# The opening loads of an attention-plus-SwiGLU kernel over two queues, batch 1's v on the GpSimd queue, and the shared tail tile moved in block 1

## The chip, the cores and the metric

The kernel runs on one core of one Trainium2 chip. The metric is device time in microseconds (us), the median of several executions. One more execution was recorded by the hardware profiler, and all views of the profile come from that one.

A core has five instruction streams: TensorE (PE, with its weight loads as PEld), VectorE (DVE), ScalarE (ACT), GpSimd (POOL) and SyncE (SP). Each stream runs in order and waits on semaphores. A DMA is issued by one of these streams and then moves its data by itself; the stream goes on.

## The reference

Linear attention with cosine weights, then an RMS norm and a SwiGLU feed-forward, in float32:

```python
# q, k, v: (8 batches, 8 heads, 576 rows, 64)
r = np.maximum(x, 0.0); phi(x) = np.concatenate([r * cos_w, r * sin_w], -1)   # 128 features
kv  = np.einsum('bhsf,bhsd->bhfd', k_p, v);  z = np.sum(k_p, axis=2)
num = np.einsum('bhsf,bhfd->bhsd', q_p, kv)
den = np.einsum('bhsf,bhf->bhs', q_p, z)[..., None] + 1e-06
x   = (num / den).transpose(0, 2, 1, 3).reshape(4608, 512)
xn  = x / sqrt(mean(x * x) + 1e-6) * rms_g
out = (silu(xn @ w_gate) * (xn @ w_val)) @ w_out      # 512 -> 1536 -> 512
```

## The kernel before

**Tiling.** Each batch has 576 rows: 512 main rows, held as four tiles of 128 rows (c or j = 0 to 3), and a tail of 64 rows. The tails of two neighbouring batches share one 128-row tile (c or j = 4). The feed-forward works in blocks: block b holds the 512 main rows of batch b, and block 8 holds all tails. A block has 12 steps n (`gval_step`, lines 663 to 670: eight 512-column matmuls for gate and value, the Silu `sg` on ACT, the product `hT` on DVE), and then 4 output steps, numbered 12 to 15 (`out_step`, lines 672 to 680: 12 matmuls with `wo`, a copy to `osb` on ACT, a store by SP). Gate and value use PSUM banks n % 2, so step n needs what ACT and DVE read in step n - 2.

**Attention of batch nb**, spread over the steps of earlier blocks: `k_phi` and `q_phi` (lines 218 to 242) scale and clip k and q, cosine half on DVE, sine half on ACT; `v_cast` (275) converts v to bf16, heads 0 to 3 (LOW) and 4 to 7 (HIGH); `kvz_pe` (293) makes kv and z, 40 matmuls in head order into PSUM tile `psA`; `kvz_evac` copies them to `kvzs`; `nd_pe` (308) makes numerator and denominator of one row tile from the transposed q (`qpT`, for the tail `qtT`); `nd_post` (331) divides, on DVE; `x_sq` squares and sums on ACT and takes the power -1/2 on POOL; `x_norm` (362) makes the bf16 `xn` on DVE; a transpose then makes `xnT`, the moving operand of the feed-forward. Transposes go through PE in the opening and for batch 1, and through DMAs issued by SP (`q_tr_dma`, 253; `x_tr_dma`, 382) from batch 2 on.

**What sets the order.** The schedule is written by hand. `at(blk, n, where, f, ...)` (line 583) hangs a piece of work on step n of block blk: "pe" ahead of that step's matmuls, "pre" after them, "post" after ACT's and DVE's part. Each engine's stream follows this order. The scheduling framework adds the semaphore waits.

**The opening** (lines 117 to 133 and 446 to 569). SP issues all loads of batch 0, in the order k LOW, k HIGH, k tail, q (row pairs 0 and 1 of 4), v LOW, v tail, v heads 4 and 5, v heads 6 and 7, q (pairs 2 and 3), `rms_g`. PE runs filler matmuls until data is there. POOL issues six weight loads (`gval_slice`, 457; they read float32 and write bf16), the first of which waits for v's tail (line 462). `kvz` of batch 0 goes to `psA`, and its first half is copied out by ACT while PE waits to go on with the second half in the same tile.

**Batch 1** (`first_loads_of_1`, 592). SP issues k, gated on the fifth weight load (594), then q, then v in two halves and its tail. POOL issues four loads of `wo`, the first gated on q (line 607). Block 0's output matmuls (717) need `wo` and are mixed with batch 1's attention.

**Batch 2** is the "late" one (lines 623 to 654): its attention runs inside block 1, the block just before it is needed. Before the change `v_cast` is at steps 3 and 4, `q_phi` with `q_tr_dma` at steps 5 to 7, `kvz` at step 7, `nd` of the four row tiles at steps 8, 10, 12 and 13, each tile's `x_norm` and transpose one step later. The shared tail of batches 0 and 1 is at step 6 (lines 734 to 743): `q_phi` of the two tails at steps 2 and 3, `nd_pe(1, 4)` at step 6. Later batches have a fixed pattern that the change leaves alone.

Of the kernel before, what the change touches and what calls it, by code (L numbers as in the profile page):

```python
# [22 lines left out]
def kernel(  # L23
# [11 lines left out]
    nc = tc.nc  # L35
# [3 lines left out]
    P = 128  # L39
# [20 lines left out]
    )  # L60
    psO = ps_open.tile([P, 2, 512], FP32, name="psO")

    nc.scalar.preload_act_table(AF.Silu)

    V, A, G = nc.vector, nc.scalar, nc.gpsimd
    LOW, HIGH = (0, 4), (4, 8)
# [1 line left out]

    raw = {}

    def load_main(which, src, b, heads=(0, 8), bufs=one):
        key = (which, b)
        if key not in raw:
            raw[key] = bufs.tile([P, H, 4 * D], FP32, name=f"r{which}", tag=f"r{which}")
        h0, h1 = heads
        return nc.sync.dma_start(  # L76
            out=raw[key][:, h0:h1, :],
            in_=src[b, h0:h1, 0:512, :].rearrange("h (p j) d -> p h (j d)", j=4),
        )

    def load_tail(which, src, b):
        t = two.tile([P, 4, D], FP32, name=f"r{which}t", tag=f"r{which}t")
        raw[(which + "t", b)] = t
        for g in range(2):
            d = nc.sync.dma_start(  # L85
                out=t[64 * g : 64 * g + 64, :, :],
                in_=src[b, 4 * g : 4 * g + 4, 512:576, :].rearrange("h s d -> s h d"),
            )
        return d
# [16 lines left out]
    def load_pair(which, b, jj):  # L106
# [5 lines left out]
        return nc.sync.dma_start(  # L112
            out=raw[key][:, :, jj * 2 * D : (jj + 1) * 2 * D],
            in_=view[:, :, 2 * jj : 2 * jj + 2, :].rearrange("p h j d -> p h (j d)"),
        )

    first = {}
    load_main("k", k, 0, LOW, two)
    load_main("k", k, 0, HIGH, two)
    load_tail("k", k, 0)  # L120
    load_pair("q", 0, 0)
    load_main("v", v, 0, LOW)
    first["v"] = load_tail("v", v, 0)
    load_main("v", v, 0, (4, 6))
    load_main("v", v, 0, (6, 8))
    load_pair("q", 0, 1)

    gb = one.tile([P, DM], FP32, name="gb")
    with nc.allow_non_contiguous_dma(reason="rms_g to all partitions"):
# [113 lines left out]

    def q_dst(b, c):
        if (b, c // 4) not in qpT:
            qpT[(b, c // 4)] = two.tile(
                [P, H, 512] if c < 4 else [P, 4, P], BF16,
                name="qpT" if c < 4 else "qtT", tag="qpT" if c < 4 else "qtT",
            )
        t = qpT[(b, c // 4)]  # L250
        return t[:, :, c * P : (c + 1) * P] if c < 4 else t[:, :, :]
# [17 lines left out]
    def copy(eng, o, i):  # L269
        if eng is nc.scalar:  # L270
            nc.scalar.copy(out=o, in_=i)  # L271
        else:
            eng.tensor_copy(out=o, in_=i)
# [19 lines left out]
    def kvz_pe(b, pst, heads=range(8)):  # L293
        o = headview(pst)
        for h in heads:
            for c in range(5):
                lhsT = kp_main[b][:, c, h, :] if c < 4 else kpt[b % 2][:, h % 4, :]
                rhs = vvm[b % 2][:, c, h, :] if c < 4 else vvt[b % 2][:, h, :]
                nc.tensor.matmul(  # L299
                    o[:, h // 4, h % 4, :], lhsT=lhsT, rhs=rhs, start=(c == 0), stop=(c == 4)  # L300
                )

    def kvz_evac(eng, b, pst, bank):
        if b not in kvzs:
            kvzs[b] = two.tile([P, 2, 4 * E], BF16, name="kvzs", tag="kvzs")
        copy(eng, kvzs[b][:, bank, :], pst[:, bank, 0 : 4 * E])

    def nd_pe(b, j, pst):

        o = headview(pst)  # L310
        for h in range(H):
            g, i = h // 4, h % 4
            if j < 4:
                nc.tensor.matmul(  # L314
                    o[:, g, i, :], lhsT=qpT[(b, 0)][:, h, j * P : (j + 1) * P],
                    rhs=kvzs[b][:, g, i * E : (i + 1) * E], start=True, stop=True,
                )
            else:
                for bb in (b - 1, b):
                    lo = 64 * (bb % 2)  # L320
                    nc.tensor.matmul(
                        o[lo : lo + 64, g, i, :],
                        lhsT=qpT[(bb, 1)][:, i, 64 * g : 64 * g + 64],
                        rhs=kvzs[bb][:, g, i * E : (i + 1) * E], start=True, stop=True,
                    )

    x_of = {}
# [129 lines left out]
    def gval_slice(c0, c1):  # L457
# [2 lines left out]

    gval_slice(0, 256)
    tc.add_manual_dep(
        weight_dmas[0].ins, first["v"].ins.name, SYNC_DEP, reason="weights after v"
    )
    gval_slice(256, 768)
    gval_slice(768, 1536)
# [8 lines left out]
    v_cast(A, 0, LOW)  # L475
    v_cast_tail(A, 0)
    filler(2, idle)
    kvz_pe(0, psA, range(0, 4))
    filler(1, idle)
    v_cast(V, 0, (4, 6))  # L480
    v_cast(V, 0, (6, 7))
    v_cast(A, 0, (7, 8))
    kvz_evac(A, 0, psA, 0)
    kvz_pe(0, psA, range(4, 6))
    filler(1, idle)
    kvz_pe(0, psA, range(6, 8))
    filler(2, idle)
    kvz_evac(V, 0, psA, 1)
    for c in (2, 3):
        q_phi(A, 0, c, 1)  # L490
    nd_pe(0, 0, psA)
# [42 lines left out]
    x_tr_pe(0, 0, psG[1][:, :])  # L534
    x_tr_evac(V, 0, 0, psG[1][:, :])
    x_norm(0, 1)
    filler(1, idle)
    open_ffn(0, (0, 1), 0, 128)
    x_tr_pe(0, 1, psG[1][:, :])
# [43 lines left out]
    def at(blk, n, where, f, *args):  # L583
        slots.setdefault((blk, n), none())[where].append((f, args))
# [7 lines left out]
    def first_loads_of_1():  # L592
        d = load_main("k", k, 1, bufs=two)
        tc.add_manual_dep(d.ins, weight_dmas[4].ins.name, SYNC_DEP, reason="after the weights")
        load_tail("k", k, 1)
        gate = load_main("q", q, 1)
        load_main("v", v, 1, LOW)
        load_main("v", v, 1, HIGH)
        load_tail("v", v, 1)
        for i in range(4):  # L600
            d = nc.gpsimd.dma_start(
                out=wo[:, 3 * i : 3 * i + 3, :],
                in_=moe_w_out[3 * i * P : 3 * (i + 1) * P, :].rearrange("(t p) m -> p t m", p=P),
            )
# [18 lines left out]
    for nb in range(2, B):  # L623
        b = nb - 1
        late = nb == 2
        for c in range(5):
            kb, kn = (b, (c + 1) // 2) if late else (b - 1, 12 + (c * 3) // 5)
            at(kb, kn, "post", k_phi, V, nb, c, 0)
            at(kb, kn, "post", k_phi, A, nb, c, 1)
            qn = 5 + (c * 3) // 5 if late else c  # L630
            at(b, qn, "post", q_phi, V, nb, c, 0)
            at(b, qn, "post", q_phi, A, nb, c, 1)
            at(b, qn, "post", q_tr_dma, nb, c)
        vb, vn = (b, 3) if late else (b - 1, 14)
# [145 lines left out]
```

## Time and profile before

| | |
|---|---|
| median of 6 runs | 339.29 us (337.63 to 340.56) |
| the profiled execution | 342.04 us, of which the recorded span is 340.3 us |
| PE busy | 323.4 us, 95% of the span |
| DVE, ACT, POOL busy | 181.3, 169.4, 37.9 us |
| mean granted TensorE clock | 0.985 of full speed |
| DMA | 54.14 MB, mean 159 GB/s |

How to read it: the 1.74 us between the profiled execution's time and its span lie outside the recorded instructions. PE's busy share counts pipelined matmuls, and a matmul at half clock is as busy as one at full clock, so 95% hides both kinds of loss; the waits of PE and the granted clock by stretch show them. Times inside the trace are counted from the start of the span. A DMA's "landing" is the time from its issue to its completion semaphore.

### The profile page before, as it was taken

Reading aid. Unit: us, or ns where it says so; the run is one execution under the profiler, and the core shown is the slowest. Engines: PE = TensorE matmul, PEld = TensorE weight load, DVE = VectorE, ACT = ScalarE, POOL = GpSimd, SP = SyncE. Lnnn points to the kernel's source line nnn. Section 1 sums busy time; section 2 is a strip of 40 time slices with the busy share of each in tenths; the row PEclk is TensorE's granted clock in tenths of the full one; section 3 lists DMA queues with packets and bytes.
Section 4 is the critical chain, followed back from the end, with each engine's and each line's share of the span. In section 5 each row is a group of like instructions: output and inputs, shape, how many; then the busy total and the mean of one; then the engine's idle time right before and its main releaser. Section 6 shows DMA issues by size and latency. Waiting matters only on the chain.

```text
span 340.3 us, 5906 instructions
## 1 busy us (share of the span) xinstructions
PE 323.4 (95%) x2157; PEld 164.4 (48%) x2193; DVE 181.3 (53%) x372; ACT 169.4 (50%) x327; POOL 37.9 (11%) x83
## 2 busy tenths in 40 slices
PE   8989999879969999999999999999999999999994
PEld 3578455535423544454445444544454444444441
DVE  4675747575842576558635765575368323304410
ACT  5655844746443645654565465546554333223321
POOL 3520302101110011101100120011001100000000
PEclk9999999989996999999999999999999999999999
DMA  8999999949693966897759776977551320020014
GB/s 232 270 206 272 266 174 280 329 116 165 164 249 79 212 163 160 209 208 193 201 153 234 175 199 152 227 180 206 151 86 35 90 77 1 2 96 27 2 31 93
DMA packets 94957, 54.14 MB, mean 159 GB/s; under 512 B 59984, under 2 KB 90192, under 8 KB 94928
## 3 DMA queue, kind: packets, MB, share of 16 engines
q1 hardware_dynamic: 90160, 49.04, 58.3%
q0 software_dynamic: 4768, 4.72, 8.4%
q8 instruction: 17, 0.28, 0.4%
q14 instruction: 12, 0.10, 0.1%
HBM read 38.01 MB, written 9.44 MB: 139 GB/s over the span
## 4 chain that ended last, share of the span: by engine, by line
PE 82%; DMA 8%; issue 2%; DVE 2%; ACT 2%; SPq 2%; POOL 0%; ACTq 0%; DVEq 0%; POOLq 0%
PE psG L403 25%; PE psV L403 25%; PE psC L423 23%; PE psA L299 3%; DMA rq<-in_q_dram 3%; PE psA L314 2%; DMA wo<-in_moe_w_out_dram 2%; DMA rv<-in_v_dram 2%; DMA xnT<-xn 1%; PE psG L423 1%; SPq L85 1%; DMA qtT<-qp 1%; SPq L76 1%; ACT scr L352 1%; DVE xt L340 1%
## 5 line engine op out<-in xcount | busy, mean ns | idle before, releaser
L418 DVE TENSOR_TENSOR hT<-psV,sg 128x512 bf16<-128x512 f32 x102 | 70.3, 690 | 107.5 <-PE psV L403 79.0
L403 PE MATMUL psG<-xnT,wg 128*128 128x512 bf16 (+1 forms) x353 | 93.2, 382 | 5.0 <-DMA xnT<-xn 3.1
L412 ACT ACTIVATE sg<-psG 128x512 f32<-128x512 f32 x102 | 60.6, 594 | 74.1 <-PE psG L403 69.0
L403 PE MATMUL psV<-xnT,wv 128*128 128x512 bf16 (+1 forms) x364 | 94.0, 380 | 0.6 <-issue 0.2
L423 PE MATMUL psC<-wo,hT 128*128 128x512 bf16 x394 | 90.8, 379 | 1.0 <-DMA wo<-in_moe_w_out_dram 0.5
L403 PEld LDWEIGHTS <-wv 128*128 128x128 bf16 x416 | 41.3, 99 | 49.3 <-issue 3.2
L423 PEld LDWEIGHTS <-hT 128*128 128x128 bf16 x432 | 41.3, 98 | 48.2 <-DMA wo<-in_moe_w_out_dram 0.6
L403 PEld LDWEIGHTS <-wg 128*128 128x128 bf16 x416 | 39.1, 99 | 46.4 <-issue 3.9
L357 POOL TENSOR_TENSOR rs<-ms,mhalf 128x1 f32<-128x1 f32 x36 | 20.0, 554 | 207.7 <-ACT scr L352 207.7
L271 ACT COPY osb<-psC 128x512 f32<-128x512 f32 x33 | 19.4, 587 | 46.8 <-PE psC L423 46.8
L352 ACT ACTIVATE scr<-xt 128x513 bf16<-128x513 f32 x36 | 22.9, 635 | 25.0 <-DVE xt L340 24.0
L364 DVE SCALAR_TENSOR_TENSOR xn<-xt,rs,gb 128x512 bf16<-128x512 f32 x36 | 27.4, 760 | 14.1 <-POOL rs L357 13.9
L340 DVE TENSOR_TENSOR xt<-psA,rec 128x512 f32<-128x512 f32 x35 | 24.2, 691 | 1.2
L212 ACT ACTIVATE qp<-rq,tab 128x512 bf16<-128x512 f32 x32 | 22.2, 712 | 2.2 <-DMA rq<-in_q_dram 2.2
L212 ACT ACTIVATE kpm<-rk,tab 128x512 bf16<-128x512 f32 (+1 forms) x34 | 21.1, 675 | 2.4 <-DMA rk<-in_k_dram 2.4
L214 DVE TENSOR_SCALAR kpm<-rk,tab 128x512 bf16<-128x512 f32 (+1 forms) x38 | 15.2, 451 | 3.2 <-DMA rk<-in_k_dram 3.2
L314 PEld LDWEIGHTS <-qpT 128*128 128x128 bf16 x256 | 12.3, 98 | 8.0 <-issue 1.4
L214 DVE TENSOR_SCALAR qp<-rq,tab 128x512 bf16<-128x512 f32 x32 | 15.2, 488 | 0.6 <-DMA rq<-in_q_dram 0.6
L443 PE MATMUL psG<-warm 128*128 128x512 bf16 x47 | 13.8, 439 | 1.2 <-DVE fidx L149 1.2
L314 PE MATMUL psA<-kvzs,qpT 128*128 128x65 bf16 x248 | 13.0, 194 | 0.6 <-DVE xt L340 0.3
L403 PE MATMUL psG<-xnt_tail,wg 128*128 128x512 bf16 x48 | 12.3, 379 | 0.1
L403 PE MATMUL psV<-xnt_tail,wv 128*128 128x512 bf16 x47 | 12.1, 379 | 0.0
(82 smaller groups left out, 191.4 us busy)
## 6 DMA issues: line engine op xcount, KB each, us to landing
out_dram<-osb SPq DMA_DIRECT2D x32, 256.0 KB, 2.8
rv<-in_v_dram SPq DMA_DIRECT2D x22, 256.0 KB, 3.5
rk<-in_k_dram SPq DMA_DIRECT2D x20, 256.0 KB, 3.4
rq<-in_q_dram SPq DMA_DIRECT2D x20, 256.0 KB, 3.1
rk<-in_k_dram SPq DMA_DIRECT2D x2, 1024.0 KB, 7.2
rq<-in_q_dram SPq DMA_DIRECT2D x2, 1024.0 KB, 9.2
rv<-in_v_dram SPq DMA_DIRECT2D x3, 512.0 KB, 9.5
wo<-in_moe_w_out_dram POOLq DMA_DIRECT2D x4, 384.0 KB, 7.2
```

Of the source, the lines that this page charges most:

```text
L212: nc.scalar.activation(out=out_ap, in_=in_ap, func=AF.Relu, scale=scale)
L214: eng.tensor_scalar(out=out_ap, in0=in_ap, scalar1=scale, scalar2=0.0, op0=ALU.mult, op1=ALU.max)
L271: nc.scalar.copy(out=o, in_=i)
L314: nc.tensor.matmul(o[:, g, i, :], lhsT=qpT[(b, 0)][:, h, j * P : (j + 1) * P], rhs=kvzs[b][:, g, i * E : (i + 1) * E], start=True, stop=True,)
L340: nc.vector.tensor_tensor(out=xt[:, 0:DM].rearrange("p (b h d) -> p b h d", b=2, d=D), in0=o[:, :, :, 0:D], in1=rec[:, :, :].unsqueeze(3). ...
L352: nc.scalar.activation(out=scr[:, :], in_=xt[:, 0 : DM + 1], func=AF.Square, scale=1.0 / math.sqrt(DM), accum_out=ms[:, :],)
L357: nc.gpsimd.tensor_tensor(out=rs[:, :], in0=ms[:, :], in1=mhalf[:, :], op=ALU.pow)
L364: nc.vector.scalar_tensor_tensor(out=xn[:, :], in0=x_of[(b, j)][:, 0:DM], scalar=rs_of[(b, j)][:, :], in1=gb[:, :], op0=ALU.mult, op1=ALU. ...
L403: nc.tensor.matmul(pst[bank][:, cols[0] : cols[1]], lhsT=w[:, t, n * P : (n + 1) * P], rhs=x[:, t, cols[0] : cols[1]], start=(t == 0), sto ...
L412: nc.scalar.activation(out=sg[:, :], in_=psG[bank][:, :], func=AF.Silu)
L418: nc.vector.tensor_tensor(out=hTs[blk][:, n, :], in0=psV[bank][:, :], in1=sg[:, :], op=ALU.mult)
L423: nc.tensor.matmul(bank, lhsT=hTs[blk][:, n, j * P : (j + 1) * P], rhs=wo[:, n, :], start=(n == 0), stop=(n == NNT - 1),)
```

## The change

Four things change together.

1. The loads of k, q and v of batch 0 are split by heads: LOW halves stay on SP's queue, HIGH halves are issued by ACT on its own queue. The loading of ACT's function table, which stood first on ACT, now follows ACT's three DMA issues. The first weight load waits for ACT's half of q instead of v's tail.
2. `kvz` of batch 0 goes to two separate PSUM banks, and both halves are copied out at the end, one by ACT and one by DVE. `kvzs` becomes two tiles per batch, with three buffers each.
3. v of batch 1 (two halves and its tail) is issued by POOL, between the second and third power instruction of batch 0's norm, instead of by SP after q. `wo` is still gated on q.
4. In block 1 batch 2 moves forward: `v_cast` to steps 2 and 3, `q_phi` with its transposes to steps 3 to 5, `kvz` to step 5, `nd` to steps 6, 8, 10 and 12. The shared tail's `nd` moves from step 6 to output step 14, with its norm and transpose at 15; `qtT` has four buffers instead of two.

The numbers of PE, DVE and ACT compute instructions are the same. In the opening SP issues 9 loads instead of 12 and ACT issues 3; four loads of batch 1 move from SP to POOL.

```diff
-    nc.scalar.preload_act_table(AF.Silu)
...
-    def load_main(which, src, b, heads=(0, 8), bufs=one):
+    def load_main(which, src, b, heads=(0, 8), bufs=one, queue=nc.sync):
...
     load_main("k", k, 0, LOW, two)
-    load_main("k", k, 0, HIGH, two)
+    load_main("k", k, 0, HIGH, two, A)
     load_tail("k", k, 0)
-    load_pair("q", 0, 0)
+    load_pair("q", 0, 0, nc.sync, LOW)
+    first["q"] = load_pair("q", 0, 0, A, HIGH)
     load_main("v", v, 0, LOW)
-    first["v"] = load_tail("v", v, 0)
-    load_main("v", v, 0, (4, 6))
-    load_main("v", v, 0, (6, 8))
+    load_main("v", v, 0, HIGH, queue=A)
+    load_tail("v", v, 0)
     load_pair("q", 0, 1)
+    nc.scalar.preload_act_table(AF.Silu)
...
-            qpT[(b, c // 4)] = two.tile(
+            qpT[(b, c // 4)] = (two if c < 4 else four).tile(
...
     tc.add_manual_dep(
-        weight_dmas[0].ins, first["v"].ins.name, SYNC_DEP, reason="weights after v"
+        weight_dmas[0].ins, first["q"].ins.name, SYNC_DEP, reason="weights after q"
     )
...
-    kvz_pe(0, psA, range(0, 4))
+    kvz_half(0, half_view[0], range(0, 4))
     filler(1, idle)
...
-    kvz_evac(A, 0, psA, 0)
-    kvz_pe(0, psA, range(4, 6))
+    kvz_half(0, half_view[1], range(4, 6))
     filler(1, idle)
-    kvz_pe(0, psA, range(6, 8))
+    kvz_half(0, half_view[1], range(6, 8))
     filler(2, idle)
-    kvz_evac(V, 0, psA, 1)
+    kvz_half_evac(A, 0, half_view[0], 0)
+    kvz_half_evac(V, 0, half_view[1], 1)
...
     x_norm(0, 1)
+    load_main("v", v, 1, LOW, queue=G)
+    load_main("v", v, 1, HIGH, queue=G)
+    load_tail("v", v, 1, G)
...
         gate = load_main("q", q, 1)
-        load_main("v", v, 1, LOW)
-        load_main("v", v, 1, HIGH)
-        load_tail("v", v, 1)
...
-            qn = 5 + (c * 3) // 5 if late else c
+            qn = 3 + c // 2 if late else c
...
-        vb, vn = (b, 3) if late else (b - 1, 14)
+        vb, vn = (b, 2) if late else (b - 1, 14)
...
-        kz, nds = (7, (8, 10, 12, 13)) if late else (4, (5, 7, 9, 11))
+        kz, nds = (5, (6, 8, 10, 12)) if late else (4, (5, 7, 9, 11))
...
-    at(1, 6, "pe", nd_pe, 1, 4, psA)
-    at(1, 6, "pre", nd_post, 1, 4, psA)
-    at(1, 6, "post", x_sq, 1, 4)
-    at(1, 7, "post", x_norm, 1, 4)
-    at(1, 7, "post", x_tr_dma, 1, 4)
+    at(1, 14, "pe", nd_pe, 1, 4, psA)
+    at(1, 14, "pre", nd_post, 1, 4, psA)
+    at(1, 14, "post", x_sq, 1, 4)
+    at(1, 15, "post", x_norm, 1, 4)
+    at(1, 15, "post", x_tr_dma, 1, 4)
```

`kvz_half` is `kvz_pe` with one bank's four heads (h % 4) in a view of `psG[1]` (LOW) or `psV[1]` (HIGH).

More of the change, by code (lines that the diff above doesn't have):

```diff
@@ L75, in load_main @@
         h0, h1 = heads
-        return nc.sync.dma_start(
+        return queue.dma_start(
             out=raw[key][:, h0:h1, :],
@@ L79, in load_main, with load_tail @@
         )
-    def load_tail(which, src, b):
+    def load_tail(which, src, b, queue=nc.sync):
         t = two.tile([P, 4, D], FP32, name=f"r{which}t", tag=f"r{which}t")
@@ L84, in load_tail @@
         for g in range(2):
-            d = nc.sync.dma_start(
+            d = queue.dma_start(
                 out=t[64 * g : 64 * g + 64, :, :],
@@ L104, in load, with load_pair @@
         last_load[(which, b)] = load_tail(which, src_of[which], b)
-    def load_pair(which, b, jj):
+    def load_pair(which, b, jj, queue=nc.sync, heads=(0, 8)):
         key = (which, b)
@@ L111, in load_pair @@
         view = src_of[which][b, :, 0:512, :].rearrange("h (p j) d -> p h j d", j=4)
-        return nc.sync.dma_start(
-            out=raw[key][:, :, jj * 2 * D : (jj + 1) * 2 * D],
-            in_=view[:, :, 2 * jj : 2 * jj + 2, :].rearrange("p h j d -> p h (j d)"),
+        return queue.dma_start(
+            out=raw[key][:, heads[0] : heads[1], jj * 2 * D : (jj + 1) * 2 * D],
+            in_=view[:, heads[0] : heads[1], 2 * jj : 2 * jj + 2, :].rearrange(
+                "p h j d -> p h (j d)"
+            ),
         )
@@ L303, in kvz_evac, with kvz_half, kvz_half_evac @@
     def kvz_evac(eng, b, pst, bank):
-        if b not in kvzs:
-            kvzs[b] = two.tile([P, 2, 4 * E], BF16, name="kvzs", tag="kvzs")
-        copy(eng, kvzs[b][:, bank, :], pst[:, bank, 0 : 4 * E])
+        kvzs[(b, bank)] = three.tile([P, 4 * E], BF16, name="kvzs", tag=f"kvzs{bank}")
+        copy(eng, kvzs[(b, bank)][:, :], pst[:, bank, 0 : 4 * E])
+    def kvz_half(b, view, heads):
+        o = view[:, 0, 0 : 4 * E].rearrange("p (h e) -> p h e", e=E)
+        for h in heads:
+            for c in range(5):
+                lhsT = kp_main[b][:, c, h, :] if c < 4 else kpt[b % 2][:, h % 4, :]
+                rhs = vvm[b % 2][:, c, h, :] if c < 4 else vvt[b % 2][:, h, :]
+                nc.tensor.matmul(
+                    o[:, h % 4, :], lhsT=lhsT, rhs=rhs, start=(c == 0), stop=(c == 4)
+                )
+    def kvz_half_evac(eng, b, view, bank):
+        kvzs[(b, bank)] = three.tile([P, 4 * E], BF16, name="kvzs", tag=f"kvzs{bank}")
+        copy(eng, kvzs[(b, bank)][:, :], view[:, 0, 0 : 4 * E])
     def nd_pe(b, j, pst):
@@ L315, in nd_pe @@
                     o[:, g, i, :], lhsT=qpT[(b, 0)][:, h, j * P : (j + 1) * P],
-                    rhs=kvzs[b][:, g, i * E : (i + 1) * E], start=True, stop=True,
+                    rhs=kvzs[(b, g)][:, i * E : (i + 1) * E], start=True, stop=True,
                 )
@@ L323, in nd_pe @@
                         lhsT=qpT[(bb, 1)][:, i, 64 * g : 64 * g + 64],
-                        rhs=kvzs[bb][:, g, i * E : (i + 1) * E], start=True, stop=True,
+                        rhs=kvzs[(bb, g)][:, i * E : (i + 1) * E], start=True, stop=True,
                     )
@@ L477 @@
     filler(2, idle)
-    kvz_pe(0, psA, range(0, 4))
+    half_view = {
+        g: t[:, :].rearrange("p (b c) -> p b c", b=1) for g, t in ((0, psG[1]), (1, psV[1]))
+    }
+    kvz_half(0, half_view[0], range(0, 4))
     filler(1, idle)
```

## The prediction

> **What bounds the kernel now.** I read the waits of PE first, since PE is busy 95% of the span and the chain of work that ended last is 82% PE. From 40 to 110 us PE waits for others only here (total us, times, longest):
>
> ```profile
> PE psG L403 <- DMA xnT<-xn: 3.1, 1, 3.1
> PE psA L321 <- DMA qtT<-qp: 2.2, 1, 2.2
> PE psG L403 <- ACT osb L271: 0.7, 1, 0.7
> PE psG L403 <- ACT xnT L271: 0.7, 1, 0.7
> PE psC L423 <- DMA wo<-in_moe_w_out_dram: 0.5, 1, 0.5
> ```
>
> The first two are block 1's: the start of block 2 waits for batch 2's last transposed tile, and the shared tail's `nd` waits for `qtT`. After block 2 starts, PE has no gap over 0.1 us. Then I read what each of the two costs beyond itself, in the table by stretch (us, then busy time and count of PE, PEld, DVE, ACT, POOL, then granted clock, DMA share, GB/s):
>
> ```profile
> 70.78:74.19 3.41, 1.18 (x14) 0.44 (x13) 2.57 (x5) 1.82 (x3) 0.00 (x0) 1.00 0.60 140
> 74.19:77.60 3.41, 3.19 (x22) 1.42 (x21) 1.06 (x3) 1.11 (x3) 0.00 (x0) 0.50 0.84 106
> 98.09:101.50 3.41, 1.29 (x6) 0.39 (x4) 0.48 (x1) 0.59 (x1) 0.00 (x0) 1.00 1.13 240
> 101.50:108.33 6.83, 5.84 (x14) 2.11 (x15) 1.09 (x2) 1.71 (x4) 0.00 (x0) 0.50 0.22 61
> 57.12:60.54 3.42, 2.68 (x21) 1.45 (x20) 3.11 (x7) 2.41 (x7) 0.85 (x2) 1.00 1.13 300
> ```
>
> A stretch of 3.41 us with PE busy 1.18 or 1.29 us is followed by half clock (0.50), one with 2.68 is not. The half clock costs 3.41 / 2 = 1.71 us after the first wait, and after the second half of the 5.83 us from 102.49, where PE resumes, to 108.32: 2.92. So the two waits cost 2.23 + 1.71 and 3.11 + 2.92, together **9.97 us**; nothing else in this kernel is as large.
>
> Third, the chain ahead of block 1 (start us, length, what):
>
> ```profile
> 29.37 9.08 DMA rq<-in_q_dram
> 38.45 0.29 issue
> 38.74 5.66 DMA wo<-in_moe_w_out_dram
> 44.40 0.05 issue
> 44.45 0.39 PE psC L423
> ```
>
> Batch 1's q lands, POOL may issue `wo`, and PE, ready at 43.98, waits 0.47. And the DMA engines, again by stretch, same columns:
>
> ```profile
> 3.00:15.00 12.00, 11.28 (x90) 5.64 (x90) 6.85 (x18) 7.47 (x15) 4.50 (x15) 1.00 1.17 302
> 15.00:29.00 14.00, 12.83 (x170) 10.57 (x171) 9.90 (x22) 7.87 (x17) 3.44 (x6) 1.00 1.23 206
> 31.00:39.00 8.00, 7.95 (x45) 4.33 (x45) 4.88 (x10) 5.23 (x10) 0.26 (x1) 1.00 1.12 323
> 40.00:42.00 2.00, 2.00 (x11) 0.87 (x9) 1.90 (x4) 2.00 (x5) 1.93 (x3) 1.00 0.71 121
> 42.00:49.30 7.30, 6.78 (x89) 4.46 (x88) 3.75 (x7) 4.03 (x6) 0.87 (x2) 1.00 1.21 196
> ```
>
> The DMA share stays above 1.1 from 3 to 40 us: the engines never run dry, so up to there a new order of loads can't finish the whole set sooner. Only 40 to 42 has room.
>
> **Part 1, opening.** The bytes are the same and the engines full, so the split over two queues only changes who lands when. k LOW landed at 4.56, k HIGH at 6.25; side by side both land near 6.2, so the first `k_phi` (4.67) starts 1.5 us later, and since DVE's ten `k_phi` (2.8 us) then run without the 0.47 us hole, q's phi starts near 9.1 instead of 8.83. ACT's three issues (SP's rows are 0.5 to 0.6 each) put its table load (1.28) at 2.5 to 3.8, ahead of k: hidden. The weights' gate moves from v's tail (11.07) to q HIGH (about 8.2); their first bytes came 2.6 us after the issue, so from 10.8 they share the engines with v LOW, v's tail, the second q and `rms_g`. At half of the 302 GB/s I get v's tail at 13.3 (11.07), the second q at 17 at the latest (14.36), `rms_g` at 18.5 (15.02; `x_norm` needed it at 18.12). ACT has that q's phi ahead of `x_sq`, so the norm chain that feeds the first weight matmul (19.84) slips by up to 1.6 us. Against it: the two `kvz` halves no longer wait for ACT's copy (0.25), and both copies run side by side (0.4). I take +1.0, bounds -1.0 (phi and copies gain, sharing is mild) and +1.6. It does not reach the sum: PE then comes to `wo` at 45.0 instead of 43.98, and waits there anyway.
>
> [...] Where the weights met SP's loads, from 29 to 30 us, the queues had 50.9% and 60.4% of the engines, near equal. [...]
>
> **Part 2, `wo`.** Now v of batch 1 stands on POOL's queue behind the weights and runs beside k and q instead of after q. POOL's four issues cost about 0.77 each (its rows are 0.76 to 0.95), 3.1 us, between the powers at 18.57 and 23.91: a hole of 4.6, hidden. The fifth weight still lands near 27.2 (same total), so k is issued then. k lands near 37 instead of 34.84; ACT has its `k_phi` ahead of step 8's `sg`, which costs PE 0.3 us or less, ahead of the `wo` wait too. q is now the last to end. The engines ran out at 40.0, and the last of v's tail, on the slowest engine, landed at 42.62: q lands between, I take 41.5. POOL issues `wo` 0.29 later. From an idle queue 256 KB of weights took 4.76 from issue to landing, 384 KB of `wo` 5.66 while v was ending: I take 5.0. So `wo` lands at 46.8 against 44.40: **+2.4**. Bounds: 40.0 + 0.29 + 4.76 = 45.05 (+0.65), and 42.62 + 0.29 + 5.66 = 48.6 (+4.2); and if v on POOL's queue ends after q, `wo` follows it there without a break: 0. PE's wait is 46.8 - 45.0 = 1.8, below the 2.1 that halved the clock; if it does halve, +1.7. SP's loads of batch 2 are gated on the third `wo` and move with it, so their distance to block 1 stays.
>
> **Part 3, block 1 up to `nd`.** Times are as before, without the shift. The tail's wait goes: -2.23 - 1.71 = **-3.94**. PE reaches `kvz` of batch 2 at step 5's start, 69.79, and needs `v_cast` LOW and then HIGH. DVE's rows in the old order (start, length):
>
> ```profile
> 67.32 0.69 DVE L418 TENSOR_TENSOR hT<-psV,sg 128x512 bf16<-128x512 f32 x1 [0.44 <-ACT sg L412]
> 67.93 0.48 DVE L214 TENSOR_SCALAR kpm<-rk,tab 128x512 bf16<-128x512 f32 x1
> 68.32 0.35 DVE L214 TENSOR_SCALAR kpt<-rkt,tab 128x256 bf16<-128x256 f32 x1
> 68.58 0.35 DVE L214 TENSOR_SCALAR qp<-rqt,tab 128x256 bf16<-128x256 f32 x1
> ...
> 71.28 0.69 DVE L273 CAST vvm<-rv 128x1024 bf16<-128x1024 f32 x1
> ```
>
> In the new order `v_cast` LOW follows at 68.58, then the tail's phi, `hT`, two q phis and `v_cast` HIGH: by start distances 0.60, 0.27, 0.60, 0.80, 0.69 it ends at 71.54. The LOW half of `kvz` keeps PE until 70.4, so PE waits about **+1.2** (bounds 0.5 and 2.0). Before, `kvz` came at 77.78 and HIGH was ready at 71.97. Behind it, the first q transpose: SP sends the tail's (1.2 to 1.3 on SP) first, then this one near 70.85; its 3.1 to 3.9 to landing give 74.0 to 74.75, and `nd` is due at 73.9: **+0.4** (0 to 0.85). k, q and v of batch 2 landed at 56.93, 65.19 and 62.4, ahead of the new slots at 64.9, 69.2 and 68.6. ACT's copies of `kvzs` (0.38 each) lie under step 5.
>
> **Part 4, start of block 2.** The last `nd` is at step 12 instead of 13 and all steps come earlier, so tile 3 has three output steps (2.6 us each) ahead of block 2. Its chain: divide 1.06, ACT behind the first `osb`, square 0.83, power 0.56, `xn` 0.74, and on SP behind the store of step 13, then 4.3 to landing. PE ends step 15 near 97.3; the store of 13 goes at 92.5, the transpose at 93.0, landing at 97.3. So the wait of 3.11 and its 2.92 of half clock go, and I leave **+0.3** (0 to 1.5). The tail's `nd` costs its 16 matmuls (0.38 at full clock) in either place; its 1.8 us of DVE, ACT's 0.83 and its SP transpose move into steps 14 and 15, where tile 3's are gone; block 8, much later, is its reader. The added buffers of `kvzs` and `qtT` add no instruction.
>
> **The sum:** +2.4 - 3.94 + 1.2 + 0.4 - 6.03 + 0.3 = **-5.67**. Against the profiled execution, 342.04 becomes 336.4; against the median of the runs, 339.29 becomes **333.6**.
>
> [...]
>
> **Rivals.** *Better:* `wo` follows v on POOL's queue without a break (0 instead of +2.4) and the waits of part 3 are at their low bounds: -8.5 to -9.9, 330.0. For it: equal shares on the queues; against it: v has half of SP's bytes. *Clock:* the waits for `wo` and at `kvz` halve the clock once each: -5.67 + 3.4 = -2.3, 337.0. For it: 1.8 and 1.2 + 0.4 are near the threshold. *Slower:* v, 1.18 MB, moves on POOL's queue at that queue's 196 to 206 GB/s instead of 323, 2.4 us more ahead of q. Then `wo` lands at 49.2 (+4.8), PE waits over 4 us and runs two stretches at half clock (+3.4), `kvz` another (+1.7): with -3.94 + 1.6 - 6.03 + 0.3 that is +1.8, 341.1. Against it: those rates are of loads that read twice the bytes they write. It decides from `wo` landing at about 49. *Not what it says:* the transposes and `v_cast` keep block 1's waits as long as they were, under other names: within 0.5%, 339.
>
> **Numbers.** Forecast 0.50 (332 to 336), better 0.15, clock 0.20 (a quarter of it within 0.5%), slower 0.10 (mostly past it), no change 0.05. A change of 0.5%, 1.7 us, is about what a measurement of this kernel can tell from none. That gives faster 0.80, same 0.10, slower 0.10. The range takes in the better rival and the clock rival with the late bounds of `wo`: 329.3 to 338.8.
>
> **What would show it.** PE's waits: no `qtT` wait, a new one at `kvz` (DVE `vvm`) near 1.2, one for `wo` near 1.8, next to none for `xnT`; the clock at 1.00 through both transitions. In the chain: `wo` landing near 46.8 with q near 41.5. Wrong if q lands before 39, if PE is not late at `kvz`, or if the clock halves at `wo`.

## The result, and the profile after

The changed kernel takes 342.05 us (median of 34 runs, 340.23 to 343.99) against 339.67 for the kernel before (69 runs, 337.41 to 341.83): ratio 1.0076, 95% interval 1.0062 to 1.0089, so about 2.6 us slower. The forecast was 333.6, faster. Ratios, here and below, come with a 95% interval and may stand a tenth of a per cent or two from the ratio of two medians.

The two profiled executions say something else: 342.04 before, 341.37 after. The profiled execution of before lies 2.37 us above the median of its kernel, that of after 0.68 below. That alone is 3.05 us of the miss, and the experiments have to say why.

The waits of PE in the changed kernel, from 5 to 110 us (total us, times, longest):

```profile
PE psG L264 <- DVE qp L216: 2.7, 1, 2.7
PE psA L329 <- DVE xt L355: 2.5, 2, 2.2
PE psC L438 <- DMA wo<-in_moe_w_out_dram: 1.3, 1, 1.3
PE psA L301 <- DVE vvm L275: 1.0, 1, 1.0
PE psG L418 <- DMA xnT<-xn: 1.0, 1, 1.0
PE psA L329 <- DMA qpT<-qp: 0.8, 1, 0.8
```

The wait for `qtT` is gone, and the wait for `xnT` fell from 3.1 to 1.0. In their place stand one for `vvm` (foreseen, 1.02), one for `qpT` (0.79), and one of 2.21 at the second `nd` of batch 2, which the forecast did not have. Block 1's waits of this kind were 2.23 + 3.11 = 5.34; now they are 1.02 + 0.79 + 2.21 + 1.00 = 5.02. **The waits were swapped, not removed.** The first line is the opening: PE's first transpose waits 2.65 us for q.

The chain of waits ahead of the first transpose (start, length, what):

```profile
2.06 7.84 DMA rkt<-in_k_dram
9.89 0.03 issue
9.92 0.02 DVEq L216
9.94 0.05 issue
9.99 0.62 DVE kpt L216
10.61 0.05 issue
10.65 0.84 DVE qp L216
```

The last of k's tail, 64 KB, took 7.84 us and landed at 9.89 (before: 7.02). The table by stretch (us, then busy time and count of PE, PEld, DVE, ACT, POOL, granted clock, DMA share, GB/s) shows what the wait does next:

```profile
8.69:12.10 3.41, 0.76 (x11) 0.50 (x10) 2.07 (x3) 1.84 (x3) 3.41 (x6) 1.00 1.18 291
12.10:15.52 3.42, 3.42 (x18) 1.74 (x16) 1.93 (x5) 2.18 (x4) 0.62 (x1) 0.50 1.28 251
```

A stretch with 0.76 us of matmuls, then one at half clock. The first weight matmul comes at 22.99 instead of 19.84.

The chain ahead of block 1, to be held against the lines shown of before:

```profile
31.23 11.67 DMA rq<-in_q_dram
42.94 0.50 issue
43.44 4.93 DMA wo<-in_moe_w_out_dram
48.37 0.05 issue
48.42 0.39 PE psC L438
```

q of batch 1 takes 11.67 us instead of 9.08 and lands at 42.90; `wo` lands at 48.37 instead of 44.40. PE, ready at 47.12, resumes 3.97 us later than before. The timeline around the 2.21 us wait (start, length, engine, line, operation; in brackets the engine's idle time and what ended it):

```profile
80.13 1.28 SPq L84 DMA_DIRECT2D rqt<-in_q_dram  x2
...
83.47 0.51 ACT L214 ACTIVATE qp<-rqt,tab 128x256 bf16<-128x256 f32 x1 [5.67 <-DMA rqt<-in_q_dram]
83.47 0.35 DVE L216 TENSOR_SCALAR qp<-rqt,tab 128x256 bf16<-128x256 f32 x1 [4.64 <-DMA rqt<-in_q_dram]
83.74 0.16 DVE L351 TENSOR_SCALAR rec<-psA 128x8 f32<-128x8 f32 x1
...
84.91 0.41 PE L329 MATMUL psA<-kvzs,qpT 128*128 128x65 bf16 x8 [2.21 <-DVE xt L355]
```

The page's label says "waits for DVE's `xt`". The row above says why DVE was late: it stood 4.64 us, and ACT 5.67, at the phi of batch 2's *tail*. That phi moved from step 7 to step 5 with the rest (`3 + c // 2` for c = 4), but SP loads this tail only at 80.13, behind the q transposes. Two streams waited in order for a tile whose reader comes far later.

### The profile page after: what moved, and what is told of

Same layout as the page of the kernel before. It is cut to its first block, busy times and chain, and to the rows that moved or that the text cites. A ratio compares the mean times of both kernels' runs of the same rounds, so it can differ in the third digit from the quotient of the medians.

```text
span 339.6 us, 5912 instructions
## 1 busy us (share of the span) xinstructions
PE 320.1 (94%) x2157; PEld 163.4 (48%) x2193; DVE 181.4 (53%) x372; ACT 169.3 (50%) x327; POOL 40.7 (12%) x87
## 4 chain that ended last, share of the span: by engine, by line
PE 77%; DMA 10%; DVE 5%; issue 3%; ACT 1%; SPq 1%; POOL 1%; DVEq 0%; ACTq 0%; POOLq 0%
PE psC L438 22%; PE psV L418 22%; PE psG L418 22%; DMA rq<-in_q_dram 3%; PE psA L301 2%; PE psA L329 2%; DMA rkt<-in_k_dram 2%; DMA wo<-in_moe_w_out_dram 1%; DMA xnT<-xn 1%; PE psG L438 1%; DMA out_dram<-osb 1%; DVE xt L355 1%; PE psG L458 1%; DVE xn L379 1%; DMA rqt<-in_q_dram 1%
## 5 line engine op out<-in xcount | busy, mean ns | idle before, releaser
L418 PE MATMUL psG<-xnT,wg 128*128 128x512 bf16 (+1 forms) x352 | 90.7, 374 | 3.0 <-DMA xnT<-xn 1.0
L418 PE MATMUL psV<-xnT,wv 128*128 128x512 bf16 (+1 forms) x366 | 92.3, 375 | 0.4
L438 PEld LDWEIGHTS <-hT 128*128 128x128 bf16 x432 | 41.2, 98 | 49.2 <-DMA wo<-in_moe_w_out_dram 1.5
L458 PE MATMUL psG<-warm 128*128 128x512 bf16 x47 | 14.8, 463 | 1.2 <-DVE fidx L151 1.2
```

Source lines behind the costliest of these rows:

```text
L418: nc.tensor.matmul(pst[bank][:, cols[0] : cols[1]], lhsT=w[:, t, n * P : (n + 1) * P], rhs=x[:, t, cols[0] : cols[1]], start=(t == 0), sto ...
L438: nc.tensor.matmul(bank, lhsT=hTs[blk][:, n, j * P : (j + 1) * P], rhs=wo[:, n, :], start=(n == 0), stop=(n == NNT - 1),)
```

## The experiments

Two theories. **A, parts add up:** every term of the sum is what the profile showed, and the miss lies in mis-sized terms (opening, `wo`, the new waits). **B, the clock:** the half clock in the profiled execution of before (10.24 us of it) is not what its usual run has, so the 4.63 us that the sum took back were mostly not there. The rival to both is that the opening is absorbed by the wait for `wo` and block 1's gain is real. The recorded expectations call the kernels e1 to e12: e1 is block 1 alone, e2 the opening alone, e3 v on POOL, e4 the tail's phi at step 7 in the changed kernel and e5 the same on e1, e6 the fillers, e7 `wo` held for k, e8 the opening's loads, e9 and e10 the two kernels towards a better version, e11 only k on two queues, e12 the weights after q. The kernels ran in three sets, each with its own runs of before (medians 338.88, 338.99 and 339.28 us); the ratios are within a set.

### Block 1 alone

The kernel before with only part 4 of the change (one `kvzs` tile of three buffers):

```diff
-            qpT[(b, c // 4)] = two.tile(
+            qpT[(b, c // 4)] = (two if c < 4 else four).tile(
...
-            qn = 5 + (c * 3) // 5 if late else c
+            qn = 3 + c // 2 if late else c
...
-        vb, vn = (b, 3) if late else (b - 1, 14)
+        vb, vn = (b, 2) if late else (b - 1, 14)
...
-        kz, nds = (7, (8, 10, 12, 13)) if late else (4, (5, 7, 9, 11))
+        kz, nds = (5, (6, 8, 10, 12)) if late else (4, (5, 7, 9, 11))
...
-    at(1, 6, "pe", nd_pe, 1, 4, psA)
+    at(1, 14, "pe", nd_pe, 1, 4, psA)
```

> The kernel before with the block 1 part alone: batch 2's v_cast, q_phi, kvz and nd at the new steps, the shared tail at step 14, qtT with four buffers, kvzs with three. Theory A (parts add up): the changed kernel's new waits in block 1 (1.0 at kvz, 0.8 and 2.2 at nd, 1.0 for xnT) appear here too and the old ones (2.23, 3.11 and 4.63 of half clock) go, so it gains 5.0 us on the profiled execution of before and 2 to 5 on the median. Theory B (clock): the unprofiled runs of before lose about 2.4 us less to the half clock than its profile, and the new waits of 5.0 replace stalls of 5.3, so the gain is 0 to 2 us on the median.

Measured: 337.45 us, ratio 0.9963 (0.9941 to 0.9985): 1.3 us faster. Against the profiled execution of before its own profile is 4.2 us shorter (337.86 to 342.04). The same edit is worth 4.2 against one execution and 1.3 against the median, which speaks for B. Its profile says more: PE runs at full clock from before block 1 to past 333 us, and from the first matmul of block 1 (60.14) to that of block 2 (101.22) it takes 41.08 us. Before's schedule at full clock (the profile of "the weights after q alone", below) takes 40.44. **At full clock this schedule gains nothing**; what it gains in the median is fewer stretches at half clock (median clock of its runs 0.9965, of before's in the same set 0.993).

### The opening alone

The kernel before with parts 1 and 2 of the change (loads split over SP and ACT, weights after q, `kvz` of batch 0 in two banks); the lines are those of the change's diff from `load_main` down to `kvz_half_evac`, without v and block 1:

```diff
-    load_main("k", k, 0, HIGH, two)
+    load_main("k", k, 0, HIGH, two, A)
...
-    kvz_pe(0, psA, range(0, 4))
+    kvz_half(0, half_view[0], range(0, 4))
```

> The opening part alone: loads split over SP and ACT, weights after q, kvz halves in two banks; v of batch 1 and block 1 as before. Theory A: the first weight matmul comes 3.1 us later (22.99 against 19.84) and PE reaches wo at 47.1, after it has landed (near 44.7), so the whole 2.5 to 3 us shows at the end. Rival: the loads through batch 1 are bound by the DMA engines, the wo wait absorbs the opening and the kernel is within 1 us of before.

Measured: 341.11 us, ratio 1.008 (1.0047 to 1.0113): 2.7 us slower. First weight matmul at 22.26 (before 19.84), no wait for `wo` left (it lands at 44.92, PE comes at 46.22). So the lateness is not absorbed when `wo` is on time.

### v of batch 1 on POOL alone

```diff
     x_norm(0, 1)
+    load_main("v", v, 1, LOW, queue=G)
+    load_main("v", v, 1, HIGH, queue=G)
+    load_tail("v", v, 1, G)
...
-        load_main("v", v, 1, LOW)
-        load_main("v", v, 1, HIGH)
-        load_tail("v", v, 1)
```

> v of batch 1 on the GpSimd queue alone, opening and block 1 as before. Theory A: q lands near 42.9 instead of 38.45 and wo near 48.4; PE, ready at 44, waits 4.4 us and the half clock adds 1.7 to 3.4, so 5 to 7 us slower. Rival (q was late only because the changed opening was): q near 41.5, wo near 46.8, 2.4 us slower, or 4.1 with the clock.

Measured: 343.56 us, ratio 1.014 (1.0104 to 1.0176): 4.7 us slower, the dearest part. k lands at 38.50 (34.84), q at 42.03 (38.45), `wo` at 47.49 (44.40). PE waits 1.41 us behind ACT's late k phi and 2.00 for `wo`, and resumes behind `wo` 3.1 us later: between the two forecasts. The clock of its runs is lower as well (median 0.989 against 0.993 for before). The opening and this part stand one beside the other, since both end at the `wo` wait: 3.15 and 3.1 became 3.97 in the whole change, not 6.25.

### The tail's phi back at step 7

The changed kernel with one line:

```diff
-            qn = 3 + c // 2 if late else c
+            qn = (7 if c == 4 else 3 + c // 2) if late else c
```

> The changed kernel with the q phi of batch 2's tail (and its transpose) put back from step 5 to step 7. Theory A: the 2.2 us wait at the second nd of batch 2 came from DVE and ACT standing at this phi until its tail load landed at 83.4; it goes, and the kernel is 2.2 us faster than the changed one, about level with before. Rival: the wait was for the q transpose itself; then it stays at 2.2 and nothing changes.

Measured: 341.58 us, ratio to before 1.008 (1.005 to 1.0109); the changed kernel has 1.0076. The 2.21 us wait is gone, as read. But `qpT` grew from 0.79 to 1.34, `xnT` from 1.00 to 1.78, and `wo` was 2.04 in that run. Between the two profiles PE's end moves by 0.86 us (334.73 to 333.87), but a gain in the medians can't be told from these intervals: the wait was largely a cover for the next one.

### The same on block 1 alone

The kernel of "block 1 alone" with the same line:

```diff
-            qn = 3 + c // 2 if late else c
+            qn = (7 if c == 4 else 3 + c // 2) if late else c
```

> The kernel before with the block-1 schedule of the change alone (as in e1), but the q phi of batch 2's tail at step 7 instead of step 5. Theory A (parts add up, the 2.27 us wait at the second output of batch 2 is pure loss): that wait goes, the others stay (kvz about 1.0, qpT 1.3 to 1.7, xnT 0.5 to 1.5): about 337.45 - 1.5 = 336.0 us. Rival (the wait only covered later ones, as e4 hinted with 0.5 us): xnT grows to 1.5 to 2 us and the median is 336.9 to 337.5.

Measured: 337.33 us, ratio 0.9934 (0.99 to 0.9967), some 1.0 us better than 0.9963, though the intervals overlap. In its profile the waits are 1.02 (`vvm`), 1.00 (`qpT`) and 2.07 (`xnT`, 0.49 before the edit): the rival's hand-over, half true.

### Fillers in the two waits

The kernel before; 9 and 13 filler matmuls of 128x512 whose results are not used:

```diff
+    at(1, 6, "pe", filler, 9, psC[0][:, :])
     at(1, 6, "pe", nd_pe, 1, 4, psA)
...
         for j in range(4):
             out_step(blk, j)
+        if blk == 1:
+            filler(13, idle)
```

> The kernel before, plus 9 filler matmuls of 128x512 ahead of the shared tail's output in block 1 and 13 after block 1's last output row; nothing else. They occupy PE in the two waits (2.23 and 3.11 us) and should hold the clock there, while the waits' ends stay where they are. Theory B (the clock's loss differs from run to run; before's profile had 10.24 us at half clock, its median run about 4.7): the profile shows no half clock at 74 and 102 us, and the median falls by 1 to 1.8 us, to 337.1 to 337.9 against a before of about 338.9 in the same job, with a narrower spread. Rival (the stretches at half clock cost 4.6 us in every run, as the prediction counted): about 334.3. Rival (clock is no cost at all outside that profile): 338.9, or more by what the fillers delay.

Measured: 337.75 us, ratio 0.9965 (0.9944 to 0.9985): 1.2 us faster (0.5 to 1.9), in the range of theory B; its runs keep within 337.25 and 338.65 while those of before spread from 337.32 to 341.16. What is left of the two waits, and the stretches behind them:

```profile
PE psA L321 <- DMA qtT<-qp: 0.5, 1, 0.5
PE psG L403 <- DMA xnT<-xn: 0.3, 1, 0.3
```

```profile
74.78:78.19 3.41, 3.41 (x64) 2.42 (x65) 2.08 (x6) 1.96 (x4) 0.00 (x0) 1.00 0.53 115
101.58:108.41 6.83, 6.83 (x32) 3.12 (x33) 3.25 (x6) 4.19 (x8) 0.00 (x0) 1.00 0.42 104
```

Both waits still end with the same DMAs, and the clock behind them is full. The rival that every run loses 4.6 us (334.3) fell. But 1.2 us is the gain net of what the fillers cost: at full clock PE's work ends at 331.98 here and at 330.55 in "the weights after q alone", 0.85 of that already at block 1, behind a longer wait for `wo`. The granted clock of each run gives a second measure. Over the 72 runs of before in the three sets, a straight line through time and clock gives 2.8 us for each 0.01 of clock, from 336.8 at full clock; the five runs at 0.999 or more took 336.81 to 337.58, the 32 at 0.990 or less 339.28 to 341.16. At the median clock, 0.9925, that is **about 2.1 us lost to the clock** (an estimate), still not 4.63, and the clock is where most of before's spread comes from.

### `wo` held for k instead of q

The changed kernel with

```diff
-        load_tail("k", k, 1)
-        gate = load_main("q", q, 1)
+        gate = load_tail("k", k, 1)
+        load_main("q", q, 1)
```

> The changed kernel, with the first quarter of wo held back for batch 1's k tail instead of for its q. If the hold for q is what makes wo late (the step of the prediction: wo lands 4.9 us after q), wo then lands at about 46 to 47 instead of 48.4 and the 1.3 us wait for it goes: 340.8 against 342.05. Rival (the engines carry the same bytes in any order): wo comes by 46 to 47, q by 44 to 45 instead of 42.9, and PE waits on the q transposes or later for as long: 342.

Measured: 339.50 us, ratio 1.001 (0.9988 to 1.0033): 2.2 us of the change's 2.6 are gone. POOL's view of `wo` in this kernel:

```profile
39.61 3.09 POOL L619 DMA_DIRECT2D wo<-in_moe_w_out_dram  x4 [12.70 <-DMA rkt<-in_k_dram]
```

`wo` goes out at 39.61 instead of 43.44 and lands at 44.51 after 4.90 us (4.93 in the changed kernel); q lands at 42.03, no later than before the edit (42.90). With v in by 36.0, the engines had room for both: the two queues' shares came to 0.81 from 39 to 43 us. The rival (the bytes take as long in any order) fell. Two reservations: 2.2 us are more than the 1.30 us wait that the edit removes, and the runs of both kernels have the same clock (0.9935 and 0.994 in the median), so 0.9 us of the gain have no account. And this execution had no half clock in the opening, and PE, which came to `wo` at 47.12 in the changed kernel, resumed at 45.29 here.

### The opening's loads alone

The kernel before with part 1's loads on two queues, the weights still held for v's tail, `kvz` as before:

```diff
-    load_main("k", k, 0, HIGH, two)
+    load_main("k", k, 0, HIGH, two, A)
     load_tail("k", k, 0)
-    load_pair("q", 0, 0)
+    load_pair("q", 0, 0, nc.sync, LOW)
+    load_pair("q", 0, 0, A, HIGH)
     load_main("v", v, 0, LOW)
+    load_main("v", v, 0, HIGH, queue=A)
     first["v"] = load_tail("v", v, 0)
-    load_main("v", v, 0, (4, 6))
-    load_main("v", v, 0, (6, 8))
```

> The kernel before, with the opening's loads alone split over the SP and ACT queues in the new order (weights still held for v's tail, kvz of batch 0 as before). Theory A: the loads alone make the late start of e2 (k's tail at 9.9 us, PE idle 2.7 us, then half clock, first weight matmul 2.4 us later): 341.1 us as e2. Rival (the halves of kvz or the earlier weights make it): first weight matmul within 0.8 us of before's 19.8 and a median of 338.9 to 339.7.

Measured: 343.60 us, ratio 1.0124 (1.009 to 1.0158): 4.2 us slower, more than the whole opening (2.7). k's tail lands at 9.50, q LOW at 10.18, v's tail at 12.67, so the weights go out at 12.97 (11.37 in before) and the fifth, which gates batch 1, lands at 29.87 (about 27.2). Releasing the weights after q gives that part back: in "the opening alone" it lands at 27.31.

### Only k on two queues

The kernel before with k HIGH alone on ACT's queue, and ACT's table load behind it:

```diff
-    load_main("k", k, 0, HIGH, two)
+    load_main("k", k, 0, HIGH, two, A)
```

> The kernel before, with only the second half of batch 0's k on the ACT queue (and the table load behind it, as in the change); q, v and the rest stay on SP in the old order. If e8's loss comes from q's and v's second halves being started at 1.25 and 1.88 us on ACT and taking the engines from k's tail, k's tail lands at 6.5 to 7.2 us here (before 7.02, e8 9.50), the first transpose starts by 9.7 and the median is 338.5 to 339.5. Rival (two queues with loads in flight as such make the short rows of k's tail slow): tail 8.5 to 9.5, first transpose 10.5 to 11, 340.5 to 342.

Measured: 339.10 us, ratio 1.0001 (0.997 to 1.0032). k's tail lands at 7.13, q at 8.76, the first transpose starts at 9.56, all as in before. Two queues as such cost nothing here; the loss comes with q's and v's halves, which start at 1.25 and 1.88 us on ACT's queue. No run takes q's split without v's. The median times from issue to landing, for loads issued in the first 3 us, first in the changed kernel:

```profile
rk<-in_k_dram SPq DMA_DIRECT2D x1, 512.0 KB, 5.0
rv<-in_v_dram ACTq DMA_DIRECT2D x1, 512.0 KB, 8.0
...
rkt<-in_k_dram SPq DMA_DIRECT2D x2, 64.0 KB, 7.3
```

and then with only k split:

```profile
rk<-in_k_dram SPq DMA_DIRECT2D x1, 512.0 KB, 4.8
...
rkt<-in_k_dram SPq DMA_DIRECT2D x2, 64.0 KB, 5.3
```

v HIGH is not needed before k and q, but moves beside k's tail and q LOW: in the changed kernel it lands at 9.84, k's tail at 9.89 and q LOW at 10.56; in before the last of v landed at 12.59, behind both.

### The weights after q alone

The kernel before with the first weight load held for its first q load instead of v's tail:

```diff
-    load_pair("q", 0, 0)
+    first["q"] = load_pair("q", 0, 0)
...
-        weight_dmas[0].ins, first["v"].ins.name, SYNC_DEP, reason="weights after v"
+        weight_dmas[0].ins, first["q"].ins.name, SYNC_DEP, reason="weights after q"
```

> The kernel before, with the weights held for q's first pair (landed 8.8) instead of v's tail (11.07). Theory (it is this edit that gives e2 back 2.2 us of what e8 lost): the weights are issued 2.3 us earlier, their fifth lands at about 25 to 26 instead of 27.2, batch 1 and wo come 1.5 to 2 us earlier, v of batch 0 lands up to 1 us later and is hidden; the median is 338 to 339, as PE hardly waits for wo in before. Rival (the weights take v's share): v's last half lands at 13.5 to 14.5 instead of 12.59, the first weight matmul is 0.5 to 1.5 us later and the median 339.5 to 340.5.

Measured: 338.88 us, ratio 0.9992 (0.9962 to 1.0022): no difference. My theory for it fell: the weights go out 2.3 us earlier and the fifth lands at 27.28, as before (about 27.2), where the DMA share was 1.07 or more in each microsecond from 3 to 40. Only where v's tail is late, as above, does this gate matter. But its profile is the clearest view of B. On stretches of 3.41 us, laid as the clock's records stand in its trace:

```profile
72.14:75.55 3.41, 1.79 (x22) 1.03 (x23) 1.98 (x6) 0.58 (x2) 0.00 (x0) 1.00 0.55 128
75.55:78.96 3.41, 3.41 (x56) 2.22 (x54) 1.48 (x3) 3.38 (x9) 0.55 (x1) 1.00 1.15 173
...
96.03:99.44 3.41, 1.43 (x7) 0.47 (x5) 0.63 (x2) 0.59 (x1) 0.00 (x0) 1.00 1.02 239
99.44:102.86 3.42, 2.70 (x13) 1.28 (x14) 0.69 (x2) 1.21 (x2) 0.00 (x0) 1.00 0.34 101
```

Its two waits are those of before, 2.22 for `qtT` and 2.70 for `xnT`, and the clock stays at 1.00 behind both. A boundary of the stretches cut each wait in two: in the stretch that holds most of it PE was busy 1.79 and 1.43 us, against 1.18 and 1.29 in before. This execution took 336.84 us, 5.2 less than the profiled one of before.

### Towards a better version

"The same on block 1 alone" plus 8 fillers:

```diff
         for j in range(4):
             out_step(blk, j)
+        if blk == 1:
+            filler(8, idle)
```

> e5 (block-1 schedule of the change alone, q phi of batch 2's tail at step 7) plus 8 filler matmuls of 128x512 after block 1's last output row, in the 2.07 us wait for block 2's xnT. If the clock is what still varies there (e5's profile has one half-clock stretch of 3.41 us at that wait, 335.4 to 338.2 us over its runs), the stretch goes and the median falls by about 1 us with a narrower spread: 335.5 to 336.3 against a before of about 339. Rival (the fillers run no faster than the wait they stand in, and delay the step behind it): 337.0 to 337.5.

Measured: 335.93 us, ratio 0.99 (0.9866 to 0.9935), within 335.35 and 336.59: the clock stayed at 1.00 and the spread closed, as expected.

The same with `wo` held for k's tail, by the two lines shown for the changed kernel:

> e9, with the first quarter of wo held back for batch 1's k tail instead of for its q. In e7 that moved wo's landing 3.86 us forward and left q where it was, but there v was already in. Here v is still behind q on SP: if the engines have room, wo lands at 41 to 42 instead of 44.4, q stays at 38.5, and as PE waits at most 1 us for wo in this kernel the gain is 0 to 0.8 us. Rival (wo takes its share from q and v): q lands at 40 to 41, v at 44 to 45, PE waits at the q transposes or kvz of batch 1, and the kernel is 1 to 2 us slower than e9.

Measured: 335.99 us, ratio 0.9895 (0.9856 to 0.9934): no gain. `wo` goes out 2.1 us earlier than without these lines (36.03 against 38.17), but takes 8.15 us and lands at 44.18 (44.55), and v's tail comes at 45.62 (42.05). Here v still moves beside it (the two queues' shares come to 1.16 from 35 to 41 us), and the bytes took as long in the new order. These two beat both kernels, that of before by 1.0% and, by the two ratios, the changed one by 1.8%.

## Why the prediction was wrong

Three steps failed. The half clock of one execution was taken for that of every run. In block 1, the wait of DVE and ACT for the data of the tail's phi was left out, so new waits replaced the old ones. And the opening, said not to reach the sum, and `wo` were sized too small. Of the 8.43 us between 333.62 and 342.05, 4.69 are terms of the sum, 3.05 the two profiled executions, 0.38 the median of before in the larger set (339.67 for 339.29), and 0.31 lies outside the terms.

Profile to profile the sum said -5.67; the end of PE's work moved by -1.02, from 335.75 to 334.73. By its steps:

- **The base.** "Against the profiled execution, 342.04 becomes 336.4; against the median of the runs ... 333.6" took the profiled execution's loss for every run's. That execution had a mean clock of 0.985; in the 72 runs of before beside the experiments it was 0.988 to 1.000, median 0.9925. 3.05 us of the miss are here: 2.37 from before's profile, 0.68 from after's. The half clock behind the two waits, "1.71" and "2.92", was sized from one execution. In the median run it is about 2.1 by the clocks on record; the fillers got 1.2 (0.5 to 1.9) of it back, net of their own cost.
- **Why it varies.** "A stretch of 3.41 us with PE busy 1.18 or 1.29 us is followed by half clock" was right, and the last section shows how right. What I left out is where the stretches lie: in the 14 profiles the first boundary on record stands anywhere from 3.87 to 6.02 us (5.92 in before, 5.28 in the changed kernel). Of the 1350 stretches counted there, those followed by half clock were the ones with 1.40 us of work or less; by that count at least 3.41 - 1.40 = 2.01 us of a wait have to fall into one stretch. For one of 2.23 us that holds in 2 x (2.23 - 2.01) + (3.41 - 2.23) = 1.62 of the 3.41 us over which its start can lie, 47%; for one of 3.11 us, 73% (estimates that take any position as likely). 0.47 x 1.71 + 0.73 x (1.71 to 2.92) is 2.1 to 2.9, some half of the 4.63 I took, and near the 2.1 from the clocks.
- **Part 1**, "+1.0, bounds -1.0 and +1.6 ... does not reach the sum": 3.15 in after's profile. I had seen k LOW's delay (it landed at 5.70; I said near 6.2) but not that k's tail and q LOW, at 9.89 and 10.56, would be last, and so not the 2.65 us wait and the half clock behind it. It was hidden behind `wo` only because that was later still; alone it is 2.7 us.
- **Part 2**, `wo` "+2.4 (bounds 0.65 and 4.2)": 3.97, 1.57 more. "I take 41.5" for q: 42.90, past the 42.62 I had as its latest; "5.0" from issue to landing: 4.93. The mechanism (q last, `wo` 5 us behind it) was right, q was mis-sized; with `wo` held for k instead, 2.2 of the 2.6 us go.
- **Part 3**: `kvz` "+1.2": 1.02, right in place and size. `qpT` "+0.4": 0.79. The 2.21 at the second `nd` was missing. I listed "the tail's phi" in DVE's new order at 0.27 us, and did not ask when `rqt` lands; its load is issued by SP behind transposes that had moved too.
- **Part 4**, `xnT` "+0.3 (0 to 1.5)": 1.00, inside the bounds. The clock stayed at 1.00 there.

The misses in after's profile, 1.57 + 2.21 + 0.39 + 0.70 - 0.18 = 4.69, are the whole distance between -5.67 and -0.98 (the sum of the terms as measured). From block 1 on, two profiles at full clock make the account short. The execution of before's schedule with full clock (the weights-after-q kernel) and the changed kernel stand at 59.72 and 63.98 at the first matmul of block 1, at 100.16 and 104.41 at that of block 2, and at 330.55 and 334.73 at PE's end: **4.2 us are lost ahead of block 1, and block 1 gives nothing back**, its waits being 4.92 and 5.02. Before's median run loses about 2.1 us to the clock that its full-clock execution does not, while the changed kernel's profile has nearly the clock of its median run (0.995 and 0.994). That leaves about 2.1, against the 2.4 between the medians and the 2.6 of the ratio.

Of the rivals, "slower" had the sign (341.1) and partly the place, `wo` after q, but not its mechanism: `wo` landed at 48.37, not 49.2, without half clock behind its 1.30 us wait. "Not what it says" had block 1's part: as long waits under other names. By the marks I set, q was not early, PE was late at `kvz`, and the clock did not halve at `wo`; it halved at the opening, which was not among them.

On the queues: the split of k alone cost nothing (1.0001), the split of k, q and v 4.2 us (1.0124), as loads that are needed later then move among those needed first (k's tail landed at 9.50 there, at 7.02 in before).

The clock also accounts for most of the 2.37 us by which before's profiled execution lies above the median: 0.985 against 0.9925 is 2.1 us by the same line, though no other run of before with its clock on record was that low. What stays open: how the 2.6 us divide between opening and `wo`, since either hides the other; what the two banks for `kvz` of batch 0 are worth, which no run takes alone; and whether the tail's phi costs the changed kernel anything (0.5 us of 2.2 in the medians, inside the spread; 0.86 between the profiles).

## What to carry to other kernels

Hold one profiled execution against the spread of runs first; if its clock is not the usual one (here 0.985, against 0.9925 in the median), a loss read from it is not a gain to be had. When a schedule moves forward, list for every moved instruction when its *data* lands, not only how long it runs: an in-order stream that stands for a tail tile delays all behind it (here DVE 4.64 us, and PE 2.21). And loads that share engines should start in the order of their need (the opening's, out of it, cost 4.2 us here); a gate that waits for another load is worth a look whenever what shares the engines with it has changed.

## What the runs showed of the hardware

**The clock.** In the trace of before the clock stands at 1.00 for 68.267 us, 0.50 for 3.413, 1.00 for 23.893 and 0.50 for 6.827: 20, 1, 7 and 2 times 3.413. Over the 14 profiles I laid this grid over each execution and counted PE's busy time. Of the 1350 stretches at full clock from the first clock record on, the 25 with 1.40 us or less were all followed by half clock (14 of them lie at the kernels' ends), and the 1325 with 1.41 or more by none. Ahead of the first record PE is slow too: in before the opening's 128x512 fillers follow each other every 0.43 us up to 5.9 us, and every 0.22 us from there. Two near the border, first with the block-1 schedule and the phi at step 7, then with v on POOL:

```profile
96.12:99.53 3.41, 1.34 (x8) 0.51 (x6) 0.75 (x1) 0.58 (x1) 0.55 (x1) 1.00 1.02 256
99.53:102.95 3.42, 3.42 (x10) 1.22 (x9) 0.62 (x2) 1.21 (x2) 0.00 (x0) 0.50 0.77 207
```

```profile
45.53:48.94 3.41, 1.41 (x14) 0.94 (x14) 2.17 (x4) 2.17 (x3) 1.19 (x3) 1.00 1.22 189
48.94:52.36 3.42, 3.42 (x57) 2.23 (x55) 0.69 (x1) 1.01 (x1) 0.00 (x0) 1.00 1.20 194
```

Of the 12 stretches at half clock, those with 2.92 us of work or more were followed by full clock; the one with 2.42 was not (in before, where the second wait therefore cost two stretches). The shortest wait of PE shown here with half clock behind it is one of 2.07 us (for `xnT`, in the first of the two stretches above).

**Queues.** With v on POOL's queue beside them, k and q of batch 1 took 11.99 and 11.67 us instead of 7.63 and 9.08 from issue to landing, and SP stood in two of its issues for 2.62 and 4.97 us, which took 0.62 and 0.61 in before. There the two halves of v, issued behind q, held it for 2.45 and 1.96 us.
